# A Fourier mixing layer and a mixture of experts on one core: where token numbers are copied, how the set-up is ordered, and what a block load waits for

## The chip, the cores and the metric

The kernel runs on one core of one Trainium2 chip. The metric is device time in microseconds (us), the median of several runs. PE is the matrix engine, DVE the vector engine, ACT the scalar engine, POOL is GpSimd, and SP is the engine that here only issues DMAs. Each engine takes its instructions strictly in the order in which the built program lists them, so one that waits holds up everything listed behind it.

## The reference

```python
B, S, D, E, F = 8, 2496, 256, 8, 1024
X = np.fft.rfft(x, axis=1)                       # x: (B, S, D)
y = np.fft.irfft(X * (filt_r + 1j * filt_i)[None], n=S, axis=1)
t = y.reshape(B * S, D)                          # 19968 tokens
logits = t @ w_gate + modality_bias[modality_id]
e_idx = np.argmax(logits, axis=1)
gate_w = softmax(logits)[np.arange(B * S), e_idx]
for e in range(E):
    mask = e_idx == e
    out[mask] = gate_w[mask, None] * (np.maximum(t[mask] @ w1[e], 0.0) @ w2[e])
```

## The kernel before

**Mixing.** Each of the eight batches goes through three matrix stages that together are the transform, the filter and the transform back. Stage 1 (`stage1`, tiles `fp`/`ps`, `t`) writes to DRAM (`b1_d`), stage 2 (`stage2`) loads it again (`load_t2`), multiplies by the filter on DVE (`p<-xf,g` with the real part `g1`, `xf<-xf,g` with the imaginary part `g2`) and by two constant matrices `a1m` and `a2m` (`pz`), and writes `z` to DRAM (`b2_d`). Stage 3 (`stage3`) loads that (`load_t4`), leaves the mixed tokens in `yo` with the token's number behind the row, and makes the router's logits.

**Routing.** For each batch `count` and `place` find every token's expert and its place in that expert's bin, `scatter` writes the rows into `bins_d` in DRAM with 20 indirect DMAs from POOL, and `table` lists on DVE which blocks of 256 rows are full by now. A round is the list of blocks that one batch's table opens: rounds 0 to 6 have 5, 10, 10, 10, 9, 10 and 10 blocks, known before the data, and the last one has the rest (15 of them in the main part, so 79 blocks in all; a branch behind it takes more where there are more).

**Experts.** For each block `load` issues on SP a DMA of 256 rows with their token numbers and gates into `xs` (five buffers, at most three blocks loaded ahead). `turn` copies the expert's `w1` into `w` and the last two words of each row into `meta` on DVE, turns the rows on PE (`pT`) and copies them on DVE into `xT`. `up` is four groups of matmuls `hps` with an ACT evacuation into `hT`; `down` is four groups into `ops`, two DVE evacuations into `osb` (three buffers; `ops` has two) and two indirect DMAs from POOL into the output. The expert steps are interleaved with the next batches' stages; up to some step of the front, `busy` matmuls that compute nothing fill PE.

**What sets the order.** The program is written with the stages interleaved by step number `n`; a scheduling layer then lists each engine's instructions and puts in the waits for data. Two of its calls matter here. `tc.issue_after(x)` puts an instruction behind `x` in the list. `free_of(ins, group)` says that `ins` need not wait for the members of `group`, because they touch other rows. Before the change a block load was not freed of the scatters (group `bins`), so it waited for every scatter that stands ahead of it in the program, those of later batches too. The set-up is listed by hand, inside `tc.manual_schedule()`.

Of the kernel before, what the change touches and what calls it, by code (L numbers as in the profile page):

```python
# [20 lines left out]
P = 128  # L21
# [7 lines left out]
def kernel(  # L29
# [202 lines left out]
    with tc.manual_schedule():  # L232
# [25 lines left out]
        nc.sync.dma_start(mb_sb, moe_modality_bias.rearrange("a e -> (a e)")[None, :])  # L258


        rows = row_int([], rows_i, "rows")
        bit0 = row_int([(ALU.bitwise_and, 1)], rows_i, "bit0")
        half = row_int([(ALU.arith_shift_right, 1)], rows_i, "half")
# [70 lines left out]
        for s0 in range(0, NS, SPB):  # L334
            for src, dst in ((w2m, a1m), (w2x, a2m)):
                tp = pp.tile([P, EV * D], F32, tag="ps", name="tp")
                for i in range(SPB):
                    nc.tensor.matmul(tp[:KB, i * KB:(i + 1) * KB], lhsT=src[:, s0 + i, :], rhs=perm,
                                     start=True, stop=True)
                ev = nc.vector.tensor_copy if dst is a1m else nc.scalar.copy  # L340
                ev(dst[:, s0:s0 + SPB, :].rearrange("p s c -> p (s c)"), tp[:KB, 0:SPB * KB])
            if s0 == 0:
                nc.vector.tensor_scalar_mul(a1m[:, 0, :], a1m[:, 0, :], wt0[:KB])
        for ga, gb in ((1, 8), (8, 16), (16, NS)):
            nc.vector.tensor_scalar_mul(g2[:, ga:gb, :], g2[:, ga:gb, :], sgn[:KB])


        zs = col("zs", lambda t: nc.vector.tensor_single_scalar(t, quart, 0.0, op=ALU.is_equal))
# [24 lines left out]
        for b in range(3):  # L373
            mv = mrawc[:, b].rearrange("p g (t two) -> p g t two", two=2)
            nc.vector.tensor_copy(mids[KA:P, :, b:NYF:3], mv[KA:P, :, 3:4 * NYG:4, 0])
        nc.vector.memset(ones_sq, 1.0)

        eio_i = const_pool.tile([P, E], I32)
        nc.gpsimd.iota(eio_i, pattern=[[1, E]], base=0, channel_multiplier=0)
# [212 lines left out]
    def scatter(g, t):  # L592

        rows = P if t < NYF else KA
        with behind("out", 1):
            ins = nc.gpsimd.indirect_dma_start(  # L596
                out=bins_d[:, :], out_offset=IOA(ap=st[g]["pos"][:rows, t:t + 1], axis=0),
                in_=st[g]["yw"][:rows, t, :], in_offset=None)

        free_of(ins, "bins")  # L600
        free_of(ins, "bin_reads")
        tc.add_to_no_dep_group("bins", ins.ins)
        paced(ins)

    def paced(ins):
        tc.add_manual_dep(ins.ins, marks["pe"][-1].name,
                          mybir.DependencyInfo(mybir.DependencyClass.Sync, mybir.DependencyReason.DATA),
                          reason="pace")
# [2 lines left out]
        tc.declare_no_dep(ins.ins, group=group, reason="disjoint rows")  # L611


    def table(K, last):

        b2 = [P, K, E]
        ni = tp_.tile([P, E], I32, tag="ni")
        av = tp_.tile([P, E], F32, tag="av")
        if last:
            ts(av, cnt, 1.0, float(BLK - 1))  # L620
            nc.vector.tensor_copy(ni, av)
        else:
            nc.vector.tensor_copy(ni, cnt)
        nc.vector.tensor_single_scalar(ni, ni, int(math.log2(BLK)), op=ALU.arith_shift_right)
        nc.vector.tensor_copy(av, ni)
        nc.vector.tensor_sub(av, av, done)
        incl = tp_.tile([P, E], F32, tag="incl")
        nc.vector.tensor_tensor_scan(incl, ones_sq[:, 0:E], av, 0.0, op0=ALU.mult, op1=ALU.add)
        excl = tp_.tile([P, E], F32, tag="excl")
        nc.vector.tensor_sub(excl, incl, av)  # L630
        v = tp_.tile([P, E], F32, tag="v")
        nc.vector.tensor_sub(v, done, excl)
        m = tp_.tile(b2, F32, tag="m")
        jb = jio[:, 0:K, None].to_broadcast(b2)
        nc.vector.tensor_tensor(m, incl[:, None, :].to_broadcast(b2), jb, op=ALU.is_le)
        ej = tp_.tile([P, K], F32, tag="ej")
        nc.vector.reduce_sum(ej, m, axis=AX.X)
        ec = tp_.tile([P, K], F32, tag="ec")
        nc.vector.tensor_scalar_min(ec, ej, float(E - 1))
        ej_i = tp_.tile([P, K], I32, tag="eji", bufs=3)  # L640
        nc.vector.tensor_copy(ej_i, ec)
        nc.vector.tensor_tensor(m, eio[:, None, :].to_broadcast(b2), ej[:, :, None].to_broadcast(b2),
                                op=ALU.is_equal)
        tmp = tp_.tile(b2, F32, tag="mt")
        nc.vector.tensor_mul(tmp, m, v[:, None, :].to_broadcast(b2))
        lb = tp_.tile([P, K], F32, tag="lb")
        nc.vector.reduce_sum(lb, tmp, axis=AX.X)
        nc.vector.tensor_add(lb, lb, jio[:, 0:K])
        bj = tp_.tile([P, K], F32, tag="bj")
        nc.vector.scalar_tensor_tensor(bj, in0=ej, scalar=float(BPE), in1=lb, op0=ALU.mult, op1=ALU.add)  # L650
        nc.vector.tensor_scalar_min(bj, bj, float(E * BPE))
        bj_i = tp_.tile([P, K], I32, tag="bji", bufs=3)
        nc.vector.tensor_copy(bj_i, bj)
        if last:
            left_i = const_pool.tile([1, 1], I32, name="left_i")
            nc.vector.tensor_copy(left_i, incl[0:1, E - 1:E])
            return ej_i, bj_i, left_i
        else:
            ts(excl, excl, -1.0, float(K))
            nc.vector.tensor_scalar_max(excl, excl, 0.0)  # L660
            nc.vector.tensor_tensor(excl, excl, av, op=ALU.min)
            nc.vector.tensor_add(done, done, excl)
            return ej_i, bj_i

    binv = bins_d.rearrange("(n p i) d -> n p i d", p=P, i=NI)

# [5 lines left out]
    def load(tab, j):  # L672

        ej_i, bj_i = tab[:2]
        with behind("ld", 2):
            bj = nc.values_load(bj_i[0:1, j:j + 1], engines=(ET.SP,), min_val=0, max_val=E * BPE)
        xs = ep.tile([P, NI, RW], I32, tag="xs", bufs=5)
        ld = nc.sync.dma_start(xs, binv[ds(bj, 1)].rearrange("o p i d -> p (o i) d"))
        tc.add_to_no_dep_group("bin_reads", ld.ins)
        marks["ld"].append(ld.ins)  # L680
        return dict(xs=xs, ej_i=ej_i[0:1, j:j + 1])
# [6 lines left out]
    def turn(b):  # L688

        xh = b["xs"].bitcast(BF16)  # L690
        with behind("w1", 1):
            ej = nc.values_load(b["ej_i"], engines=(ET.DVE,), min_val=0, max_val=E - 1)
        b["w1"] = ep.tile([P, DC, F], BF16, tag="w1", name="w1")
        cp = nc.vector.tensor_copy(b["w1"].rearrange("p a f -> p (a f)"),  # L694
                              w1sb[:, ds(ej, 1)].rearrange("p o a f -> p (o a f)"))
        marks["w1"].append(cp.ins)
        b["xT"] = ep.tile([P, DC, NI, P], BF16, tag="xT", name="xT")

        b["meta"] = ep.tile([P, NI, 2], I32, tag="meta", bufs=8, name="meta")
        nc.vector.tensor_copy(b["meta"], b["xs"][:, :, DW:DW + 2])  # L700
        pT = op.tile([P, DC, NI, P], BF16, tag="tr")
        for dc in range(DC):
            for i in range(NI):
                nc.tensor.transpose(pT[:, dc, i, :], xh[:, i, dc * P:(dc + 1) * P], ident)  # L704
        nc.vector.tensor_copy(b["xT"], pT)  # L705
        b["hT"] = ep.tile([P, FT, NI * P], BF16, tag="hT", name="hT")

    FQ = 2
# [142 lines left out]
    while True:  # L851
        for g in range(1, B):
            if 0 <= n - begin[g] < NP:
                input_piece(g, n - begin[g])
        for g in range(B):
            k = n - begin[g] - OFF2
            if (k + LEAD) % 4 == 0 and 0 <= k + LEAD < NS // EV:
                load_t2(g, (k + LEAD) // 4)
            if 0 <= k <= NS // EV:
                stage2(g, k)  # L860
        for g in range(B):
            k = n - begin[g] - OFF3
            if (k + LEAD) % 3 == 0 and 0 <= k + LEAD < NPY:
                load_t4(g, (k + LEAD) // 3)
            if 0 <= k <= NPY + 1:
                stage3(g, k)
            if k == NPY + 2:
                count(g)
            if k == NPY + 3:
                place(g)  # L870
                tabs[g] = table(KR[g], g == B - 1)
                to_bins.append([g, 0])
        alone[0] = n < FRONT
        if alone[0]:
            busy(10 if n < NP + 18 else 4)
        left = 2 if n < begin[B - 1] + OFF3 + NPY + 3 else NY
        left = pace(pace(left) if n < FRONT + 10 else left)
        if n >= WSTART and n % 3:
            load_w()
        owed += STEPS  # L880
        while owed >= 1:
            owed -= 1
            outs = len(marks["out"])
            moe.step()
            if len(marks["out"]) == outs:
                left = pace(left)
        n += 1
        if not to_bins and n > begin[B - 1] + OFF3 + NPY + 4:
            break
    LAG = 0  # L890
    while moe.step():
        pass
    left = nc.values_load(tabs[B - 1][2], min_val=0, max_val=LEFT)  # L893
    for p0, p1 in zip(PARTS[1:], PARTS[2:]):
        with tc.If(left > p0):
            for m in marks.values():
# [35 lines left out]
```

## Time and profile before

| | |
|---|---|
| median of 3 runs | 711.7 us (709.67 to 718.71) |
| the profiled execution | 709.73 us, its span 707.6 us |
| PE busy | 580.3 us, 82% of the span |
| DVE, ACT, POOL busy | 369.9, 379.9 and 365.8 us |
| mean granted TensorE clock | 0.913 of full speed |

The span runs from the first to the last instruction; 2.1 us lie around it. Busy time counts work and not the waits between. The granted clock takes two values, 1.0 (2.4 GHz) and 0.5 (1.2 GHz), so a mean between them says how much of a stretch ran at each. Times in a timeline count from the start of the span.

### The profile page before, as it was taken

What the parts mean: (1) busy time and instruction counts of PE and PEld (TensorE: products, weight loads), DVE (VectorE), ACT (ScalarE), POOL (GpSimd) and SP (SyncE); (2) the same over time, 40 slices, a digit from 0 to 9 for tenths busy, and PEclk for the clock granted to TensorE, in tenths of its full rate; (3) what the DMA queues carried; (4) which work ended last, traced back from release to release, by engine and by line L of the source; (5) the groups of instructions that cost most, each with busy time, mean ns of one, the idle gap of its engine ahead of it and who ended that gap; (6) DMA issues with size and microseconds to landing.
All of it is one profiled execution on the core that took longest, in us unless ns stands there. A gap on an engine that the chain in (4) does not pass through costs nothing. (4 is left out here: it accounts for less than half of the span.)

```text
span 707.6 us, 16119 instructions
## 1 busy us (share of the span) xinstructions
PE 580.3 (82%) x4966; PEld 485.0 (69%) x4966; DVE 369.9 (52%) x1225; ACT 379.9 (54%) x672; POOL 365.8 (52%) x409
## 2 busy tenths in 40 slices
PE   3738678796997899898989979899869359999990
PEld 2527566565776688686878868687658249999990
DVE  8252134574655656564486557456446135555540
ACT  4414455564575577674767746454435126666660
POOL 8002111175376367376647727756766755555451
PEclk9969778898799699998999999899999799999996
DMA  9969889997767767656675565344223333333320
GB/s 154 227 132 201 178 226 210 224 244 180 187 177 176 188 165 184 191 132 179 161 194 151 160 168 136 116 112 137 91 89 107 103 104 102 106 113 101 97 76 20
DMA packets 84222, 106.08 MB, mean 150 GB/s; under 512 B 12164, under 2 KB 66250, under 8 KB 83980
## 3 DMA queue, kind: packets, MB, share of 16 engines
q0 software_dynamic: 21504, 50.75, 29.7%
q1 hardware_dynamic: 62632, 54.23, 29.1%
q8 instruction: 48, 0.79, 0.5%
q14 instruction: 38, 0.31, 0.1%
HBM read 71.07 MB, written 52.74 MB: 175 GB/s over the span
## 5 line engine op out<-in xcount | busy, mean ns | idle before, releaser
L720 ACT ACTIVATE hT<-hps 128x512 f16<-128x512 f32 x316 | 188.3, 597 | 174.6 <-PE hps L715 173.6
L715 PE MATMUL hps<-xT,w 128*128 128x256 f16 x1264 | 208.6, 286 | 33.5 <-DVE xT L705 33.2
L737 POOL DMA_INDIRECT out_dram<-osb,meta x158 | 158.5, 1003 | 126.6 <-DVE osb L735 73.1
L596 POOL DMA_INDIRECT bins_d<-yo,pos_i x160 | 162.1, 1013 | 77.9 <-issue 31.1
L728 PE MATMUL ops<-w2sb,hT 128*128 x1264 | 197.3, 279 | 0.3 <-issue 0.2
L715 PEld LDWEIGHTS <-w 128*128 128x128 f16 x1264 | 146.4, 148 | 45.8 <-DVE xT L705 36.1
L728 PEld LDWEIGHTS <-hT 128*128 128x128 f16 x1264 | 126.2, 100 | 15.7 <-issue 0.6
L700 DVE COPY meta<-xs 128x4 int32<-128x4 int32 x79 | 14.8, 188 | 120.5 <-DMA xs<-bins_d 110.6
L477 ACT CAST xf<-ps 104x512 f16<-104x512 f32 x96 | 56.2, 585 | 34.4 <-PE ps L464 32.2
L479 DVE TENSOR_TENSOR p<-xf,g 104x512 f16<-104x512 f16 x96 | 40.5, 422 | 63.8 <-ACT xf L477 63.4
L735 DVE TENSOR_SCALAR osb<-ops,meta 128x256 f32<-128x256 f32 x158 | 69.3, 475 | 5.5 <-PE ops L728 5.5
L694 DVE COPY w<-w1sb 128x2048 f16 x79 | 55.3, 700 | 28.5 <-PE hps L715 26.1
L486 ACT CAST z<-pz 104x512 f16<-104x512 f32 x96 | 56.6, 590 | 23.3 <-PE pz L473 12.5
L472 PE MATMUL pz<-p,a1m 104*104 104x256 f16 x192 | 52.2, 290 | 12.1 <-DVE p L479 4.1
L464 PE MATMUL ps<-t,w2m 104*104 104x256 f16 x192 | 41.1, 299 | 24.7 <-DMA t<-b_d 21.4
L473 PE MATMUL pz<-xf,a2m 104*104 104x256 f16 x192 | 51.0, 289 | 0.2 <-DVE xf L480 0.2
L824 PE MATMUL busy<-ident 128*128 128x256 f16 x296 | 50.9, 310 | 0.0
L205 ACT CAST t<-fp 96x512 f16<-96x512 f32 x57 | 32.3, 583 | 33.6 <-PE fp L200 19.8
L705 DVE COPY xT<-pT 128x512 f16<-128x512 f16 x79 | 33.1, 419 | 19.9 <-PE pT L704 19.5
L464 PEld LDWEIGHTS <-w2m 104*104 104x104 f16 x192 | 24.7, 139 | 26.4 <-issue 21.4
L533 DVE COPY yT<-lt 128x512 f16<-128x512 f16 x80 | 33.5, 419 | 17.0 <-PE lt L529 14.1
L480 DVE TENSOR_TENSOR xf<-xf,g 104x512 f16<-104x512 f16 x96 | 40.2, 419 | 2.2 <-DVE p L479 0.3
(194 smaller groups left out, 716.5 us busy)
## 6 DMA issues: line engine op xcount, KB each, us to landing
xs<-bins_d SPq DMA_DIRECT2D x79, 130.0 KB
t<-b_d SPq DMA_DIRECT2D x24, 416.0 KB
b_d<-z SPq DMA_DIRECT2D x48, 208.0 KB
xt<-in_x_dram POOLq DMA_DIRECT2D x24, 384.0 KB
b_d<-t SPq DMA_DIRECT2D x48, 192.0 KB
t<-b_d SPq DMA_DIRECT2D x24, 384.0 KB
w1sb<-in_moe_w_dram POOLq DMA_DIRECT2D x16, 256.0 KB
w2sb<-in_moe_w_dram POOLq DMA_DIRECT2D x8, 512.0 KB
```

The costliest lines, as they stand in the source:

```text
L464: mm = nc.tensor.matmul(ps[:KB, i, :], lhsT=w2m[:, s + i, :], rhs=st[g]["t2", s // SCH][:, s % SCH + i, :], start=True, stop=True)
L472: nc.tensor.matmul(pz[:KB, i, :], lhsT=a1m[:, s_ + i, :], rhs=p1[:, i, :], start=True, stop=False)
L473: nc.tensor.matmul(pz[:KB, i, :], lhsT=a2m[:, s_ + i, :], rhs=p2[:, i, :], start=False, stop=True)
L477: nc.scalar.copy(xf, ps[:KB])
L486: nc.scalar.copy(st[g]["z"][:, kk % 2], pz[:KB])
L596: ins = nc.gpsimd.indirect_dma_start(out=bins_d[:, :], out_offset=IOA(ap=st[g]["pos"][:rows, t:t + 1], axis=0), in_=st[g]["yw"][:rows, t, ...
L694: cp = nc.vector.tensor_copy(b["w1"].rearrange("p a f -> p (a f)"), w1sb[:, ds(ej, 1)].rearrange("p o a f -> p (o a f)"))
L715: mm = nc.tensor.matmul(hps[:, k, :], lhsT=b["w1"][:, dc, ft:F:FT], rhs=b["xT"][:, dc].rearrange("p i t -> p (i t)"), start=(dc == 0), sto ...
L720: nc.scalar.activation(b["hT"][:, q * FQ:(q + 1) * FQ, :], hps, AF.Relu)
L728: nc.tensor.matmul(b["ops"][:, i, :], lhsT=b["hT"][:, ft, i * P:(i + 1) * P], rhs=w2sb[:, ds(b["ej"], 1), ft, :], start=(ft == 0 and i == ...
L735: nc.vector.tensor_scalar_mul(osb[:, i, :], b["ops"][:, i, :], gate[:, i, :])
L737: ins = nc.gpsimd.indirect_dma_start(out=out[:, :], out_offset=IOA(ap=b["meta"][:, i, 0:1], axis=0), in_=osb[:, i, :], in_offset=None, bou ...
```

## The change

Four edits. In the set-up, `ones_sq` is filled as the first of the hand-listed DVE instructions and no longer near their end; and the sign `sgn`, which was multiplied into `g2` on DVE in three instructions, is put on the rows of `a2m` instead, by the ACT copies that write `a2m` out of PSUM anyway (the first slot keeps a plain copy, so one copy becomes two). In `turn`, the `meta` copy stands behind the `xT` copy and not ahead of it. And a block load of the round that batch g opened is freed of the scatters of the batches after g; the last round waits for all, as before.

```diff
+        nc.vector.memset(ones_sq, 1.0)
         rows = row_int([], rows_i, "rows")
...
-                ev = nc.vector.tensor_copy if dst is a1m else nc.scalar.copy
-                ev(dst[:, s0:s0 + SPB, :].rearrange("p s c -> p (s c)"), tp[:KB, 0:SPB * KB])
+                if dst is a1m:
+                    nc.vector.tensor_copy(dst[:, s0:s0 + SPB, :].rearrange("p s c -> p (s c)"),
+                                          tp[:KB, 0:SPB * KB])
+                    continue
+                a = 0
+                if s0 == 0:
+                    nc.scalar.copy(dst[:, 0, :], tp[:KB, 0:KB])
+                    a = 1
+                nc.scalar.activation(dst[:, s0 + a:s0 + SPB, :].rearrange("p s c -> p (s c)"),
+                                     tp[:KB, a * KB:SPB * KB], AF.Copy, scale=sgn[:KB])
...
-        for ga, gb in ((1, 8), (8, 16), (16, NS)):
-            nc.vector.tensor_scalar_mul(g2[:, ga:gb, :], g2[:, ga:gb, :], sgn[:KB])
...
-        nc.vector.memset(ones_sq, 1.0)
...
+        tc.add_to_no_dep_group("bins%d" % g, ins.ins)
...
         ld = nc.sync.dma_start(xs, binv[ds(bj, 1)].rearrange("o p i d -> p (o i) d"))
+        for h in range(tab[2] + 1, B):
+            free_of(ld, "bins%d" % h)
...
-        b["meta"] = ep.tile([P, NI, 2], I32, tag="meta", bufs=8, name="meta")
-        nc.vector.tensor_copy(b["meta"], b["xs"][:, :, DW:DW + 2])
         pT = op.tile([P, DC, NI, P], BF16, tag="tr")
...
-        nc.vector.tensor_copy(b["xT"], pT)
+        turned = nc.vector.tensor_copy(b["xT"], pT)
+        b["meta"] = ep.tile([P, NI, 2], I32, tag="meta", bufs=8, name="meta")
+        with tc.issue_after(turned.ins):
+            nc.vector.tensor_copy(b["meta"], b["xs"][:, :, DW:DW + 2])
```

The order tables below are of the built programs: line, operation, output and inputs, shape. In the first, DVE's list in the last round's neighbourhood, where batch 7 is scattered; before:

```order
L735 TENSOR_SCALAR osb<-ops,meta 128x256 x2
L692 TENSOR_LOAD ej_i
L692 ISA x2
L700 COPY meta<-xs 128x4
L705 COPY xT<-pT 128x512
L700 COPY meta<-xs 128x4
L694 ISA
L694 COPY w_9594<-w1sb 128x2048
L735 TENSOR_SCALAR osb<-ops,meta 128x256 x2
L692 TENSOR_LOAD ej_i
L692 ISA x2
L700 COPY meta<-xs 128x4
```

and after:

```order
L745 TENSOR_SCALAR osb<-ops,meta 128x256 x2
L701 TENSOR_LOAD ej_i
L701 ISA x2
L712 COPY xT<-pT 128x512
L715 COPY meta<-xs 128x4
L703 ISA
L703 COPY w_9592<-w1sb 128x2048
L745 TENSOR_SCALAR osb<-ops,meta 128x256 x2
L701 TENSOR_LOAD ej_i
L701 ISA x2
L712 COPY xT<-pT 128x512
L715 COPY meta<-xs 128x4
```

Before, a `meta` copy stands one or two blocks ahead of the `xT` copy of its own block; now it stands right behind it, everywhere.

The second is SP's list in the same place, each block load with its waits (DMASW are the semaphores of POOL's DMAs, the scatters among them; DMAHW those of SP's own; PE and DVE free the `xs` buffer). Before:

```order
L678 DMA xs_9418<-bins_d 128x260 [waits DMASW4_49,DMASW3_49,DMASW5_49,DMASW0_49,DMAHW1_49,DVE_49,PE_49]
L676 TENSOR_LOAD bj_i_7091
L676 ISA x2
L751 TENSOR_LOAD end_i_9719
L751 ISA x2
```

and after:

```order
L685 DMA xs_9416<-bins_d 128x260 [waits DMAHW4_49,DMAHW7_49,DVE_49,PE_49]
L683 TENSOR_LOAD bj_i_7089
L683 ISA x2
L685 ISA
L685 DMA xs_9515<-bins_d 128x260 [waits DMAHW0_49,DVE_49,PE_49]
```

The DMASW waits are gone from this load; in the whole list they are left on the first load of each round.

The third is DVE's list in the set-up; before:

```order
L341 CAST a1m<-tp 104x416 x5
L345 TENSOR_SCALAR g_69<-g_69,sgn 104x1792
L345 TENSOR_SCALAR g_69<-g_69,sgn 104x2048 x2
L348 TENSOR_SCALAR zs<-quart 128x1
L349 TENSOR_TENSOR zri<-zs,bit_147 128x1
```

and after, where `g_69` is `g2`:

```order
L371 TENSOR_SCALAR wbm<-wb_400,j0w 96x48
L372 TENSOR_SCALAR wbm<-wb_400,j1w 96x48
L486 TENSOR_TENSOR xf<-xf,g_69 104x512 x2
L377 CAST mids<-mraw 96x8x6 x3
L378 CAST mids<-mraw 96x8x2
```

The first DVE instruction that needs `g2` was ahead of all the small constants, and of `ones_sq`; now it is the filter's own product, with the first stage-2 evacuations ahead of it and about half of the constants (`eio` among them) still behind.

## Rows read from the trace of the kernel before

**Rows 1.** The page's busy table: busy us, share of the span, instructions.
```profile
PE 580.3 (82%) x4966; PEld 485.0 (69%) x4966; DVE 369.9 (52%) x1225; ACT 379.9 (54%) x672; POOL 365.8 (52%) x409
```

**Rows 2.** Waits over the whole span: us in total, times, longest us.
```profile
DVE meta L700 <- DMA xs<-bins_d: 110.6, 41, 8.0
...
PE ps L464 <- DMA t<-b_d: 21.4, 5, 8.7
```

**Rows 3.** Waits of SP's queue over the whole span.
```profile
SPq L678 <- DMA bins_d<-yo,pos_i: 189.3, 54, 15.1
...
SPq L678 <- PE pT L704: 57.4, 26, 3.2
```

**Rows 4.** Waits of PE from 237 to 580 us.
```profile
PE hps L715 <- DVE xT L705: 33.2, 9, 10.9
PE pz L472 <- DVE yo L539: 3.5, 1, 3.5
PE pz L472 <- DVE lg L542: 2.5, 1, 2.5
PE ps L464 <- DVE lg L542: 2.2, 1, 2.2
PE lt L524 <- DVE yo L539: 1.9, 1, 1.9
```

**Rows 5.** Timeline, 540 to 561 us: start, us, instruction, idle before it.
```profile
546.97 0.38 PE L704 MATMUL pT<-ident,xs 128*128 128x128 f16 x4
...
549.89 0.17 DVE L700 COPY meta<-xs 128x4 int32<-128x4 int32 x1 [6.05 <-DMA xs<-bins_d]
...
557.00 0.35 SPq L678 DMA_DIRECT2D xs<-bins_d  x1
...
559.44 0.17 DVE L700 COPY meta<-xs 128x4 int32<-128x4 int32 x1 [7.96 <-DMA xs<-bins_d]
559.52 0.42 DVE L705 COPY xT<-pT 128x512 f16<-128x512 f16 x1
...
560.00 1.07 PE L715 MATMUL hps<-xT,w 128*128 128x256 f16 x4 [10.89 <-DVE xT L705]
```

**Rows 6.** Busy time by stretch, the granted clock (PEclk) and the DMA share behind it.
```profile
554.40:564.60 10.20, 4.61 (x24) 3.55 (x25) 1.88 (x5) 1.19 (x2) 7.92 (x8) 0.50 0.27 80
...
sum 41.00, PE 34.47 PEld 25.76 DVE 24.54 ACT 13.32 POOL 22.16; mean PE 4.31 PEld 3.22 DVE 3.07 ACT 1.66 POOL 2.77
...
sum 17.20, PE 11.61 PEld 9.02 DVE 7.00 ACT 3.58 POOL 10.38; mean PE 3.87 PEld 3.01 DVE 2.33 ACT 1.19 POOL 3.46
```

**Rows 7.** The same by batch: PE, PEld, DVE, ACT, POOL, each with its instructions.
```profile
301.40:366.70 65.30, 60.41 (x513) 49.27 (x512) 38.14 (x133) 41.51 (x75) 40.09 (x42) 0.92 0.66 168
...
483.50:537.50 54.00, 44.47 (x409) 36.11 (x408) 28.44 (x106) 22.43 (x38) 35.76 (x36) 0.97 0.26 82
537.50:577.00 39.50, 21.54 (x177) 18.15 (x174) 11.25 (x36) 11.94 (x20) 29.57 (x30) 0.87 0.36 111
```

**Rows 8.** The same for a stretch of experts alone.
```profile
590.00:680.00 90.00, 90.00 (x864) 84.53 (x862) 49.00 (x117) 57.04 (x96) 46.42 (x49) 1.00 0.32 102
```

**Rows 9.** What POOL waited for, 537.5 to 577 us.
```profile
POOL bins_d L596 <- issue: 2.1, 7, 0.3
```

**Rows 10.** Timeline of the set-up.
```profile
41.55 2.01 DVE L345 TENSOR_SCALAR g<-g,sgn 104x1792 f16<-104x1792 f16 x3 [11.92 <-DMA g<-g]
...
47.45 0.60 PE L409 MATMUL mb_ps<-mb_sb,ones_sq 1*128 1x16 f32 x2 [12.31 <-DVE ones_sq L376]
...
47.68 1.11 POOL L435 DMA_DIRECT2D w1sb<-in_moe_w_dram  x2 [12.97 <-DVE eio L381]
...
51.21 0.42 PE L473 MATMUL pz<-xf,a2m 104*104 104x256 f16 x1
```

**Rows 11.** Busy time by stretch around the end of the set-up.
```profile
44.00:48.00 4.00, 0.56 (x3) 0.52 (x3) 3.32 (x26) 0.80 (x2) 0.32 (x1) 0.50 0.00 0
...
53.00:142.00 89.00, 67.94 (x535) 54.98 (x532) 32.95 (x100) 45.72 (x84) 14.50 (x28) 0.85 0.97 208
```

More of the change, by code (lines that the diff above doesn't have):

```diff
@@ L611, in free_of, with table @@
         tc.declare_no_dep(ins.ins, group=group, reason="disjoint rows")
-    def table(K, last):
+    def table(g, K, last):
         b2 = [P, K, E]
@@ L656, in table @@
             nc.vector.tensor_copy(left_i, incl[0:1, E - 1:E])
-            return ej_i, bj_i, left_i
+            return ej_i, bj_i, B - 1, left_i
         else:
@@ L662, in table @@
             nc.vector.tensor_add(done, done, excl)
-            return ej_i, bj_i
+            return ej_i, bj_i, g
     binv = bins_d.rearrange("(n p i) d -> n p i d", p=P, i=NI)
@@ L870 @@
                 place(g)
-                tabs[g] = table(KR[g], g == B - 1)
+                tabs[g] = table(g, KR[g], g == B - 1)
                 to_bins.append([g, 0])
@@ L892 @@
         pass
-    left = nc.values_load(tabs[B - 1][2], min_val=0, max_val=LEFT)
+    left = nc.values_load(tabs[B - 1][3], min_val=0, max_val=LEFT)
     for p0, p1 in zip(PARTS[1:], PARTS[2:]):
```

## The prediction

> **What bounds the kernel now.** I read the page first, then the waits, then the stretches where they lie. PE is busy 82% of the span, far more than any other engine [rows 1]; so time is gained where PE stands still or runs slowly, and nowhere else. The list of waits shows that the largest wait for data on DVE is the `meta` copy for its block load: 110.6 us in 41 times [rows 2]. SP has the cause: its block loads wait 189.3 us in 54 times for scatters into the bins [rows 3]. Neither engine is the bound, so these sums are not time yet. What they cost is in PE's own waits from 237 to 580 us: 33.2 us in nine waits for an `xT` copy and four single ones of 3.5, 2.5, 2.2 and 1.9 us behind other DVE instructions, 43.3 us together [rows 4].
>
> The timeline shows how one arises [rows 5]. PE turned the rows of a block at 546.97; their `xT` copy needed nothing more. But DVE's list has the `meta` copies of two later blocks ahead of it. The second one's load went out at 557.00, once scatters of batch 7 had landed that this block does not hold, and its `meta` ran at 559.44, after 7.96 us of standing. `xT` followed at 559.52, and PE began again at 560.00 after 10.89 us. The turned block had been there for 12 us.
>
> A stop costs more than itself. In the eight stretches of half clock that stand beside these stops, PE was busy for 34.47 us at a granted clock of 0.5, which is 17.2 us lost; three of the eight lie behind 483.5 us, with 11.61 us busy, so 5.8 us of the 17.2 are there and 11.4 before [rows 6].
>
> **The bins.** A block load of rounds 0 to 6 no longer waits for scatters of later batches; the order table shows the waits gone. It adds no instruction. What is left to wait for is the `xs` buffer, and the first load of each round, which waits for its own batch. The loads go out early, three blocks ahead; a block lasts 3.75 us where only experts run (864 matmuls in 90 us, 36 for a block, so 24 blocks) [rows 8], so a load has some 11 us of cover, and one that had nothing to wait for took 2.4 us to its `meta` (557.00 to 559.44) [rows 5].
>
> Against this edit speaks a rule of the Trainium skill, DMA: Bandwidth & Descriptors, section Issuing engines are not separate DMA queues: transfers from SP and POOL run on the same 16 DMA engines and interleave, so loads that no longer wait for scatters run beside them. From rows the engines are 66% busy in one batch's stretch and 26 and 36% in the last two [rows 7], so there is room, and a load would have to take over four times its 2.4 us to be seen: by the rows this costs 0. [...]
>
> **The `meta` copy** moves behind `xT`. It takes what stood ahead of `xT` away, so that even a late load stops only its own block. Both edits remove the same stops; I count them once. The copy is 0.17 us [rows 5], 79 of them 13.4 us. It used to run while DVE waited anyway; now it can hold the next DVE instruction up. Bounds: 0 and 13.4 us. DVE is busy 38.14 of 65.30 us in a full batch [rows 7], so most of it stays hidden; I take 3. It also frees `xs` 0.6 us after the turn and not before it, which the cover of three blocks hides.
>
> **The stops removed, in two parts.** The last two stretches, 483.5 to 577 us, have PE idle for 54.00 − 44.47 = 9.5 and 39.50 − 21.54 = 18.0 us [rows 7], 27.5 together; so 43.3 − 27.5 = 15.8 us of the DVE stops lie earlier.
>
> *Early, 237 to 483.5:* 15.8 us of stops and 11.4 us of clock, 27.2 us. Is another engine next? In the fullest batch POOL has 42 instructions, 40.09 us [rows 7], and 0.3 us between two even where it is never idle [rows 9]: 40.1 + 12.6 = 52.7 us of 65.3. PE's 60.41 us at a mean clock of 0.92 are 55.6 at full clock [rows 7]. POOL is close but below. I take all 27.2.
>
> *Late, 483.5 to 577:* PE could give 27.5 + 5.8 = 33.3 us, but POOL holds that up. Its 36 and 30 instructions need 35.76 + 10.8 = 46.6 and 29.57 + 9.0 = 38.6 us, 85.2 of the 93.5 us: it can gain 8.3 [rows 7, 9]. Beyond that PE can only run ahead of the output DMAs. `osb` has three buffers and `ops` two, so `down` of a block may begin when the output of the fifth block before it has left; in the trace it is the block just before. That lead is four blocks of 3.75 us, 15.0 us, and POOL works it off later, when a block costs it less than PE (46.42 us busy of 90, [rows 8]). So 8.3 + 15.0 = 23.3 us, the smaller of the two.
>
> **The set-up.** `ones_sq` is filled early, and the three sign products go (2.01 us on DVE, behind 11.92 us of waiting for the copied half of `g2`). Now PE waits 12.31 us for `ones_sq`, since every small constant is listed behind those products [rows 10]. With them gone PE goes on to stage 2 when its load lands; but the filter's product with `g2` cannot begin before 41.55, when `g2` is there. Today the first `pz` from it is at 51.21. So at most 51.21 − 41.55 = 9.7 us. The lower bound is 0: stage 1 of batch 1 is now listed behind those first stage-2 matmuls. The row nearest to the value is that of the DMA engines: 97% busy from 53 to 142 us, and idle from 44 to 48 [rows 11], because the weight loads wait for `eio`, 12.97 us [rows 10]. Where transfers bound the next 89 us, the idle 4.0 us is what an earlier start gives. I take 4. The added ACT copy costs nothing: ACT is busy 0.80 us in those 4 [rows 11].
>
> **The sum** against the profiled execution's 709.7 us (2.0 below the median, within the runs' scatter): 27.2 + 23.3 + 4.0 − 3.0 = 51.5, which gives 658 us.
>
> **The rivals.**
>
> *POOL binds and gives no lead.* If an output DMA's landing is late, or DVE stops at an `osb` copy whose buffer has not come free, and stops with it `xT` behind it, the 15.0 us of lead go: 658 + 15 = 673 us. For it: POOL does not rest from 537.5 to 577 beyond the 0.3 us between instructions. Against: five buffers lie between the two.
>
> *The stops move.* The first load of a round still waits for its batch's scatters, which a busy POOL does late, and SP holds the `z` stores and stage loads behind it. If half of the stops comes back so, 25 of the 50.5 us: 658 + 25 = 683 us. For it: PE already waits 21.4 us for stage loads [rows 2]. Against: blocks are queued up when a round opens.
>
> *Slower.* The loads now reach SP's front early and wait there for an `xs` buffer; in the trace such waits are up to 3.2 us, 57.4 in all [rows 3], mostly in the last stretch where nothing is behind them. If they stood in front of stage stores and loads twice in each of six batches, each would cost a stage-load wait of 4.3 us (21.4 in 5, [rows 2]) and as much half clock as the stops had on average, 17.2 of 43.3 or 1.7 us: 12 × 6.0 = 72 us, 658 + 72 = 730 us. It decides when a load's buffer comes free later than the next `z` is ready. Against: the block five before is turned two blocks before the load is listed.
>
> That the change does not do what it says is excluded by the order table.
>
> **How the numbers follow.** The forecast has 0.53, POOL without lead 0.25, stops that move 0.15, slower 0.05, and 0.02 something else. Faster by over 2%, below 697 us, holds the first two, most of the third and nothing of the fourth: 0.88. Within 2%, about what a measurement can tell from no change, 0.07; slower 0.05. Range: the lower end takes the set-up's full 9.7 (5.7 more), no cost of the `meta` copy (3) and all 33.3 of the late stops (10): 640. The upper end is the case of moved stops with the set-up's 0 (4 us) and 3 more for `meta`: 690.
>
> **What would show it.** Of the waits: DVE's `meta` for `xs` near zero, SP's waits for scatters down to the first load of each round, PE's for `xT` a few us. Of the stretches: full clock from about 240 us on; POOL without rest over the last two batches, and `osb` or `out_dram` waits there if it binds. In the set-up: no wait for `ones_sq`, the first `pz` at 42 to 46 us, no empty DMA stretch. I am wrong if PE's idle time between 240 and 580 us stays above 30 us, or if POOL's share says that it could not go faster.

## The result and the profile after

The changed kernel takes 675.6 us (median of 4 runs, 669.94 to 689.98) where the kernel before takes 711.4 in the same comparison: a ratio of 0.945, 95% interval 0.9345 to 0.9559. The ratio is taken from the runs within 1.5% of each kernel's fastest, so it is not quite that of the two medians. The profiled execution is 669.94 us, its span 668.2. The range of 640 to 690 holds it; the forecast of 658 is 12 us too low against the profiled execution (18 against the median), and the time lies next to the rival in which POOL gives no lead (673).

The page's busy table answers to [rows 1]; PE has 565.7 us of work where it had 580.3, with the same number of instructions, because less of it runs at half clock (the mean granted clock is 0.928, it was 0.913):

```profile
PE 565.7 (85%) x4966; PEld 475.1 (71%) x4966; DVE 370.7 (55%) x1222; ACT 379.7 (57%) x673; POOL 367.8 (55%) x409
```

Three milestones split the gain: the first scatter of batch 2, the first of batch 6, and the end of PE's last matmul. Before they stand at 237.1, 483.5 and 690.3 us, after at 237.4, 462.7 and 650.9. So the front lost 0.3, the early stretch gained 21.1 (246.4 to 225.3) and the late one 18.6 (206.8 to 188.2); the sum, 39.4, is the whole difference of the spans.

PE's waits from 237 to 580 us, which answer to [rows 4]: 43.3 us there behind DVE, here 18.9 in all, and none above 4.3.

```profile
PE hps L725 <- DVE xT L712: 11.0, 6, 3.7
PE ps L517 <- ACT t L205: 4.3, 1, 4.3
PE psO L578 <- DVE c L569: 2.1, 3, 0.8
PE ops L738 <- issue: 1.5, 5, 0.5
```

SP's waits over the whole span answer to [rows 3]. The block loads still stand 172.6 us, but now for the `xs` buffer, which the `meta` copy frees; for scatters they wait five times, about once for each round's first load. The `meta` wait for `xs`, 110.6 us in [rows 2], has no row any more. In its place DVE has a new one, the last line here (of the list of all engines):

```profile
SPq L685 <- DVE meta L715: 172.6, 54, 7.8
...
SPq L685 <- DMA bins_d<-yo,pos_i: 16.5, 5, 8.6
...
DVE osb L745 <- DMA out_dram<-osb,meta: 23.0, 7, 6.9
```

The stretches answer to [rows 7]: us, then PE, PEld, DVE, ACT and POOL with their instructions, granted clock, DMA share, GB/s. The first one is the whole early part, the last one the early part of the kernel before. In the second and third, POOL's work and 0.3 us for each of its instructions are 36.4 + 11.1 = 47.5 of 47.4 us and 31.5 + 9.6 = 41.1 of 40.9: it never rests.

```profile
237.40:462.70 225.30, 217.53 (x1981) 181.58 (x1980) 154.44 (x521) 154.06 (x278) 149.95 (x153) 0.98 0.66 176
...
462.70:510.10 47.40, 46.13 (x445) 38.74 (x444) 33.30 (x121) 24.47 (x43) 36.41 (x37) 1.00 0.35 104
510.10:551.00 40.90, 30.97 (x246) 26.14 (x243) 13.04 (x34) 16.50 (x28) 31.45 (x32) 0.87 0.35 111
...
237.10:483.50 246.40, 228.50 (x1979) 187.57 (x1978) 151.36 (x523) 155.32 (x279) 149.66 (x152) 0.94 0.61 162
```

Where the late time stays is seen in three timelines of 519 to 529 us, DVE's, POOL's and PE's (start, us, instruction, idle before it). POOL issues the two output DMAs of a block at 523.44 and 524.73, after four scatters in a row; the `osb` copies wait 5.66 us for that buffer and begin at 527.28. `xT`, whose block had been turned at 522.90, stands behind them and runs at 528.23, and PE goes on at 528.71 after 3.67 us.

```profile
519.61 0.88 DVE L745 TENSOR_SCALAR osb<-ops,meta 128x256 f32<-128x256 f32 x2 [2.42 <-DMA out_dram<-osb,meta]
...
527.28 0.88 DVE L745 TENSOR_SCALAR osb<-ops,meta 128x256 f32<-128x256 f32 x2 [5.66 <-DMA out_dram<-osb,meta]
528.23 0.42 DVE L712 COPY xT<-pT 128x512 f16<-128x512 f16 x1
...
522.17 0.97 POOL L602 DMA_INDIRECT bins_d<-yo,pos_i  x1 [0.30 <-issue]
523.44 0.98 POOL L747 DMA_INDIRECT out_dram<-osb,meta  x1 [0.30 <-PE pT L711]
524.73 0.98 POOL L747 DMA_INDIRECT out_dram<-osb,meta  x1 [0.30 <-DMA bins_d<-yo,pos_i]
...
522.90 0.38 PE L711 MATMUL pT<-ident,xs 128*128 128x128 f16 x4
...
528.71 1.07 PE L725 MATMUL hps<-xT,w 128*128 128x256 f16 x4 [3.67 <-DVE xT L712]
```

The windows with half clock that are left behind 237 us answer to [rows 6]; 14.47 us busy there where it was 34.47:

```profile
295.70:302.50 6.80, 5.17 (x24) 3.37 (x24) 3.54 (x20) 2.75 (x5) 3.88 (x4) 0.50 0.73 225
527.80:534.60 6.80, 5.89 (x30) 4.55 (x31) 1.48 (x4) 1.79 (x3) 5.28 (x6) 0.50 0.25 78
538.00:541.40 3.40, 3.40 (x21) 2.64 (x19) 0.23 (x1) 1.19 (x2) 2.48 (x4) 0.51 0.29 82
sum 17.00, PE 14.47 PEld 10.56 DVE 5.25 ACT 5.73 POOL 11.64; mean PE 4.82 PEld 3.52 DVE 1.75 ACT 1.91 POOL 3.88
```

In the set-up the steps came as foreseen, and without their fruit. These are stretches that answer to [rows 11], and four instructions that answer to [rows 10], of PE's, DVE's and POOL's timelines. The first `pz` from `g2` is at 42.83 (it was at 51.21), and the DMA engines no longer stand empty from 44 to 48; but their idle time has only been spread over 36 to 53 us. The weight loads go out at 48.36, later than before (47.68), and `eio` is cast at 47.85 (before, at 47.42), with the filter's products ahead of it on DVE. The load of the next `xt` has to wait 23.96 us for PE's stage 1, which now stands behind stage 2's first matmuls, and goes out at 42.35; before it did at 34.12.

```profile
36.00:44.00 8.00, 7.33 (x51) 5.86 (x50) 1.37 (x8) 2.98 (x6) 0.59 (x1) 0.77 0.77 142
44.00:48.00 4.00, 4.00 (x39) 3.75 (x38) 1.97 (x8) 2.48 (x6) 0.00 (x0) 1.00 0.53 121
48.00:53.00 5.00, 4.96 (x46) 4.52 (x44) 4.09 (x23) 3.67 (x8) 3.74 (x7) 1.00 0.72 116
53.00:142.00 89.00, 59.66 (x452) 46.50 (x450) 28.87 (x88) 39.84 (x74) 12.09 (x23) 0.81 0.94 205
...
42.83 0.27 PE L479 MATMUL pz<-xf,a2m 104*104 104x256 f16 x1 [0.67 <-DVE xf L486]
...
47.85 0.17 DVE L387 CAST eio<-eio_i 128x8 f32<-128x8 int32 x1
...
42.35 0.59 POOL L137 DMA_DIRECT2D xt<-in_x_dram  x1 [23.96 <-PE fp L200]
48.36 1.11 POOL L441 DMA_DIRECT2D w1sb<-in_moe_w_dram  x2 [5.43 <-DVE xf L486]
```

### The profile page after: what moved, and what is told of

Same layout as the page of the kernel before. It is cut to its first block, busy times and chain, and to the rows that moved or that the text cites. A ratio compares the mean times of both kernels' runs of the same rounds, so it can differ in the third digit from the quotient of the medians.

```text
span 668.2 us, 16107 instructions
## 1 busy us (share of the span) xinstructions
PE 565.7 (85%) x4966; PEld 475.1 (71%) x4966; DVE 370.7 (55%) x1222; ACT 379.7 (57%) x673; POOL 367.8 (55%) x409
## 4 chain that ended last, share of the span: by engine, by line
PE 54%; DMA 20%; issue 10%; POOL 5%; DVE 5%; ACT 3%; POOLq 0%; SPq 0%; DVEq 0%; ACTq 0%
PE hps L725 15%; PE ops L738 13%; DMA t<-b_d 7%; DMA b_d<-t 7%; POOL out_dram L747 5%; PE ps L517 4%; PE ps L518 4%; PE lt L530 3%; PE busy L834 3%; DMA bins_d<-yo,pos_i 2%; PE pz L479 2%; PE pz L478 2%; PE ps L470 2%; PE pT L711 2%; DMA g<-g 2%
## 5 line engine op out<-in xcount | busy, mean ns | idle before, releaser
L730 ACT ACTIVATE hT<-hps 128x512 f16<-128x512 f32 x316 | 188.3, 597 | 144.6 <-PE hps L725 143.5
L725 PE MATMUL hps<-xT,w 128*128 128x256 f16 x1264 | 203.5, 281 | 11.1 <-DVE xT L712 11.0
L747 POOL DMA_INDIRECT out_dram<-osb,meta x158 | 160.6, 1016 | 91.4 <-DVE osb L745 43.1
L738 PE MATMUL ops<-w2sb,hT 128*128 x1264 | 193.8, 276 | 1.5 <-issue 1.5
L738 PEld LDWEIGHTS <-hT 128*128 128x128 f16 x1264 | 124.8, 99 | 15.7 <-issue 2.3
L478 PE MATMUL pz<-p,a1m 104*104 104x256 f16 x192 | 50.4, 282 | 6.6 <-DVE p L485 6.3
L479 PE MATMUL pz<-xf,a2m 104*104 104x256 f16 x192 | 48.9, 280 | 2.1 <-DVE xf L486 1.9
L470 PEld LDWEIGHTS <-w2m 104*104 104x104 f16 x192 | 24.0, 136 | 37.1 <-issue 27.2
L518 PEld LDWEIGHTS <-wbm 96*32 96x32 f16 x160 | 14.8, 93 | 39.4 <-issue 30.1
```

The source lines that it names most:

```text
L470: mm = nc.tensor.matmul(ps[:KB, i, :], lhsT=w2m[:, s + i, :], rhs=st[g]["t2", s // SCH][:, s % SCH + i, :], start=True, stop=True)
L478: nc.tensor.matmul(pz[:KB, i, :], lhsT=a1m[:, s_ + i, :], rhs=p1[:, i, :], start=True, stop=False)
L479: nc.tensor.matmul(pz[:KB, i, :], lhsT=a2m[:, s_ + i, :], rhs=p2[:, i, :], start=False, stop=True)
L725: mm = nc.tensor.matmul(hps[:, k, :], lhsT=b["w1"][:, dc, ft:F:FT], rhs=b["xT"][:, dc].rearrange("p i t -> p (i t)"), start=(dc == 0), sto ...
L730: nc.scalar.activation(b["hT"][:, q * FQ:(q + 1) * FQ, :], hps, AF.Relu)
L738: nc.tensor.matmul(b["ops"][:, i, :], lhsT=b["hT"][:, ft, i * P:(i + 1) * P], rhs=w2sb[:, ds(b["ej"], 1), ft, :], start=(ft == 0 and i == ...
```

## The experiments

Ratios are to the kernel before on the same chip, with 95% intervals; the first four runs shared one chip, the next four another, and the last two pairs one each.

### One part of the change at a time

**The set-up alone** (`e1_setup`): the kernel before with the first four pieces of the diff, up to the second `ones_sq` line, and nothing else.

> The kernel before with the two set-up edits alone. Theory (the front is bound by the bytes it moves, and no load starts earlier): the first scatter stays at 142 us within 1 us and the time within 3 us of before, ratio 0.997 to 1.003. Rival (the forecast's term): 4 us less, 0.994 or lower, with the first scatter at 138 us or earlier.

Measured: 715.83 us beside 713.16, ratio 1.003 (0.9981 to 1.0081), the `xT` stops still 30.6 us in 7. Alone it gains nothing, and the interval leaves out the rival's 0.994. The first scatter, at 146.7 us, is where neither expectation had it: 5 us later than the 141.7 of the kernel before, in one execution each (more on this moment below).

**The `meta` copy alone** (`e2_meta`):

```diff
-        b["meta"] = ep.tile(...)
-        nc.vector.tensor_copy(b["meta"], b["xs"][:, :, DW:DW + 2])
...
+        turned = nc.vector.tensor_copy(b["xT"], pT)
+        b["meta"] = ep.tile(...)
+        with tc.issue_after(turned.ins):
+            nc.vector.tensor_copy(b["meta"], b["xs"][:, :, DW:DW + 2])
```

> The kernel before with the meta copy behind the xT copy alone; the block loads still wait for all scatters ahead of them. Theory (DVE's place in line is what stopped PE, the late loads stop it only once the three blocks ahead are used up): most of the gain up to batch 6, 15 to 21 us, and some 7 us in the last two batches: 23 to 29 us less, ratio 0.959 to 0.968. Rival (the load's wait is the cause): PE's stops move to the turned rows and under 10 us are gained, 0.985 or higher.

Measured: 691.49 us, ratio 0.972 (0.9621 to 0.9822), some 20 us, between the two expectations. PE's waits from 237 to 580 us have no `xT` stop. PE now stops one step earlier, where it turns a block whose load is late (first line); the loads still stand for scatters (second line, of SP's).

```profile
PE pT L702 <- DMA xs<-bins_d: 15.0, 5, 5.6
...
SPq L678 <- DMA bins_d<-yo,pos_i: 172.0, 53, 10.0
```

So with the copy out of the way a late load still costs PE: 15.0 us here, in five stops. The prediction's "stops only its own block" put no price on that.

**The freed loads alone** (`e3_bins`):

```diff
         tc.add_to_no_dep_group("bins", ins.ins)
+        tc.add_to_no_dep_group("bins%d" % g, ins.ins)
...
+        for h in range(tab[2] + 1, B):
+            free_of(ld, "bins%d" % h)
```

> The kernel before with the block loads freed alone; meta stays ahead of xT. Theory (either edit removes the same stops, since a load that goes out early has landed when its meta copy is listed): 34 to 40 us less, ratio 0.944 to 0.953, DVE's wait of meta for xs under 15 us. Rival (both are needed): meta still waits over 50 us and under 20 us are gained, 0.972 or higher.

Measured: 693.42 us, ratio 0.975 (0.9653 to 0.9849), some 18 us. My theory that either edit alone removes the stops fell here. The rival's two numbers came. The wait for scatters is down to 19.6 us in 6, but the `meta` copy, still ahead of `xT`, stands 73.6 us (it was 110.6), for something new: `meta` has eight buffers, and the one that it needs is still to be read by output DMAs that have not run. PE's `xT` stops stay at 14.1 us in 7.

```profile
DVE meta L703 <- DMA out_dram<-osb,meta: 73.6, 31, 7.4
...
PE hps L718 <- DVE xT L708: 14.1, 7, 3.8
```

**The freed loads with 24 `meta` buffers** (`e7_metabufs`), to see whether that row is the cause:

```diff
-        b["meta"] = ep.tile([P, NI, 2], I32, tag="meta", bufs=8, name="meta")
+        b["meta"] = ep.tile([P, NI, 2], I32, tag="meta", bufs=24, name="meta")
```

> The kernel before with the freed block loads alone, as in the earlier run of that edit, and 24 buffers for meta instead of 8. Theory (with loads early, the meta copy stands ahead of the xT copy only because its eight buffers wait for output DMAs, 73.6 us in 31): that wait falls below 10 us, and the edit then does nearly all that both do, a ratio to the kernel before of 0.945 to 0.958. Rival (the meta copy ahead of the xT copy meets some other late thing): the meta copy waits as long for something else, and the ratio stays at 0.970 to 0.980.

Measured: 676.35 us, ratio 0.942 (0.9378 to 0.947), as good as the whole change. The `meta` wait for output DMAs has no row; what is left of the copy's waiting for its load is below, with the `osb` wait that the whole change has too:

```profile
DVE osb L738 <- DMA out_dram<-osb,meta: 20.9, 4, 6.9
DVE meta L703 <- DMA xs<-bins_d: 15.6, 11, 4.0
```

So the freed loads are enough for the whole gain, on condition that the `meta` copy doesn't stop DVE for its own buffer. Moving the copy and giving it buffers are two ways to that, equal within their intervals.

### The late stretch

**A fourth `osb` buffer** (`e4_osb`), with `xs` cut from five to four for room:

```diff
-        xs = ep.tile([P, NI, RW], I32, tag="xs", bufs=5)
+        xs = ep.tile([P, NI, RW], I32, tag="xs", bufs=4)
...
-        osb = ep.tile([P, NI, D], F32, tag="osb", bufs=3)
+        osb = ep.tile([P, NI, D], F32, tag="osb", bufs=4)
```

> The changed kernel with four osb buffers for three, and four xs buffers for five to make room. Theory (the late stops come from DVE standing at an osb copy whose buffer is still being written out, with the xT copy behind it): one more block of lead, 3 to 6 us less than the changed kernel, DVE's osb wait for output DMAs down from 23.0 us to under 18, PE's stops at xT down from 11.0 us. Rival (POOL's rate alone sets that stretch, buffers do not matter): the same time within 2 us. With four xs buffers costing something: up to 3 us more.

Measured: 669.89 us, ratio 0.936 with a wide interval (0.9164 to 0.9559): in the direction expected, and not to be told from the whole change by that alone. DVE's `osb` wait is 17.7 us in 5 and PE's `xT` stops are 8.0 us in three, both down as expected.

**The last batch's scatters spread** (`e5_spread`), two for each block in place of about five:

```diff
+    steps = 0
...
-        left = pace(pace(left) if n < FRONT + 10 else left)
+        tail = n >= begin[B - 1] + OFF3 + NPY + 3
+        if not tail:
+            left = pace(pace(left) if n < FRONT + 10 else left)
...
-            if len(marks["out"]) == outs:
+            steps += 1
+            if len(marks["out"]) == outs if not tail else steps % 2 == 0:
                 left = pace(left)
```

> The changed kernel, with the scatters of the last batch listed at two for each block of experts instead of about five. Theory (in the last round osb's copies wait for output DMAs that stand behind clumps of scatters on POOL, and hold the xT copy behind them): the xT stops of PE behind 510 us, 10.2 us in four, fall below 4, and the half clock beside them, 4 to 5 us lost, mostly goes; the ratio to the kernel before falls from 0.945 to 0.925 to 0.935. Rival (POOL's rate sets the time whatever the order): PE stands still elsewhere, and the ratio stays at 0.940 to 0.950.

Measured: 673.83 us, ratio 0.938 (0.9327 to 0.944), between the two expectations; the interval touches the ratio of the whole change. The stops did not go: eight of them, 9.6 us together, the `osb` wait 21.9 us in 8. The clumps alone are not the cause.

**Both** (`e8_best`):

> The changed kernel with the last batch's scatters spread as in the run beside it, and four osb and four xs buffers. If the spreading takes the stops and the fourth buffer takes what is left (alone it gave a ratio to the kernel before of 0.936), a ratio of 0.920 to 0.930; if both take the same stops, that of the better of the two, 0.930 to 0.937; if POOL's rate binds, 0.936 to 0.945.

Measured: 661.18 us, ratio 0.920 (0.9148 to 0.9258), the best version. From the first scatter of batch 7 to PE's end it takes 131.8 us; the whole change takes 140.8, the spread scatters 137.6 and the fourth buffer 137.4, in one execution each. So the two together give more than either alone, which the ratio says too: its interval lies below that of the spread scatters and that of the whole change (the fourth buffer's is too wide to tell). PE's waits from 470 to 600 us and the last two scatter stretches:

```profile
PE hps L725 <- DVE xT L712: 5.9, 4, 2.3
...
464.40:512.30 47.90, 46.76 (x450) 39.31 (x448) 33.92 (x124) 24.98 (x44) 36.96 (x36) 1.00 0.33 102
512.30:564.50 52.20, 47.25 (x442) 43.00 (x442) 24.09 (x60) 29.23 (x49) 40.30 (x39) 1.00 0.41 122
```

POOL rests as little as before (40.3 + 11.7 = 52.0 of 52.2 us). What changed is the order of its work and how far PE may run ahead of it: PE is busy 47.3 of 52.2 us there, at full clock (30.97 of 40.9 us in the whole change).

### The front

**Eight more weight loads** (`e6_twice`):

```diff
+            if q < DC and e < E // 2:
+                paced(nc.gpsimd.dma_start(w1sb[:, E - 1 - e, q], moe_w1[e, q * P:(q + 1) * P, :]))
             if q < DC:
                 ins = nc.gpsimd.dma_start(w1sb[:, e, q], moe_w1[e, q * P:(q + 1) * P, :])
```

> The changed kernel, with eight more weight loads of 256 KB in the front, the same data into places that a later load fills again. Theory (the front is bound by its transfers, so an earlier start of PE gains nothing there): 2.1 MB at the rate of the stretch from 53 to 142 us, 208 GB/s, put the first scatter 8 to 10 us later than the 142.4 of the changed kernel, and the whole time is 7 to 10 us longer, a ratio to the kernel before of 0.955 to 0.960. Rival (the front is bound by its chain of waits, transfers have room): first scatter within 3 us of 142.4 and the ratio within 0.940 to 0.950.

Measured: 683.41 us, ratio 0.952 (0.9465 to 0.9581), 5 us above the whole change's ratio, though the two intervals overlap; first scatter at 152.0, where three kernels with nothing added on the same chip have 144.6, 148.3 and 148.6. The DMA share from 53 to 142 us went to 1.00:

```profile
53.00:142.00 89.00, 56.11 (x418) 43.71 (x417) 24.78 (x68) 33.93 (x63) 15.26 (x30) 0.81 1.00 210
```

2.1 MB, some 10 us of transfer, cost about 5 by either measure (4.8 us from the mean of those three): about half of it seems to have found room. Neither expectation holds whole.

**Half of the weights not loaded** (`e9_half`), the places of experts 4 to 7 filled with zeros on POOL, so that those experts' outputs are zero:

```diff
-            if q < DC:
+            if e >= E // 2:
+                ins = nc.gpsimd.memset(w1sb[:, e, q] if q < DC else w2sb[:, e], 0.0)
+            elif q < DC:
```

> The changed kernel without the weights of experts 4 to 7: their places are filled with zeros by POOL and not loaded, so 4.2 MB fewer come in the front, and the outputs of those experts are zero. Theory (the front is bound by its transfers): the engines' share from 53 to 142 us was 0.94 and 4.2 MB are 20 us at 208 GB/s; the first scatter comes 8 to 20 us earlier than in the changed kernel and its kin (142 to 148 us), and the whole time is 8 to 20 us shorter, a ratio to the kernel before of 0.917 to 0.934. Rival (the chain of stores, loads and copies from stage to stage sets the front's length): first scatter at 140 or later and a ratio of 0.938 to 0.948.

This run and the next fell on a chip where the kernel before takes 791.75 us (below), so its ratio, 0.975 (0.9697 to 0.9798), doesn't compare with those above. The front does: first scatter at 135.7 us, where kernels that load all their weights on the two slower chips have 140.2, 141.2 and 145.1. The share from 53 to 142 us is 0.83:

```profile
53.00:142.00 89.00, 64.09 (x477) 50.37 (x475) 33.17 (x110) 41.89 (x77) 23.94 (x29) 0.78 0.83 187
```

Not all of the 4.2 MB would have come before the first scatter. Up to that moment this kernel moved 24.6 MB (135.7 us at 181 GB/s, first line) and `e10_nosetup`, with all its weights on the same chip, 27.3 MB (141.2 us at 193 GB/s):

```profile
0.00:135.70 135.70, 90.00 (x668) 73.67 (x668) 58.24 (x206) 65.32 (x118) 39.48 (x67) 0.88 0.85 181
...
0.00:141.20 141.20, 90.59 (x664) 73.83 (x665) 60.56 (x209) 64.61 (x117) 32.88 (x68) 0.85 0.93 193
```

So the 20 us of the expectation are some 13 there (2.7 MB at 208 GB/s), and they bring the batch 4 to 9 us forward, at the low end of the theory or below it. Transfers are a part of the front's bound. That the chain from stage to stage is the rest is likely and not shown.

### The set-up again, and two slower chips

**The best version without the set-up's edits** (`e10_nosetup`; then `e11_without`, with `e12_with` beside it, the best version itself). The edit is the diff's set-up part, taken out.

> The kernel with spread scatters and four osb and four xs buffers, without the set-up's edits. Theory (they are worth nothing, since they bring no transfer forward): the same as with them, a ratio to the kernel before of 0.915 to 0.926. Rival (they were hidden by noise or by the stops that stand behind, and are worth the 4 us of the forecast): 0.926 to 0.932.

> The same kernel as in the earlier run without the set-up's edits (spread scatters, four osb and four xs buffers), beside the one with them on the same chip. Theory (the set-up's edits bring no transfer forward and are worth nothing): the two medians within 0.5% of each other, some 3.5 us, and the first scatters within 4 us. Rival (worth the 4 us of the forecast or more): this one 4 us or more above the other, and its first scatter as much later.

> The kernel with spread scatters, four osb and four xs buffers and all edits of the change, beside the one without the set-up's edits. [...] Rival: 4 us or more below the other.

Measured: `e10_nosetup` 779.72 us beside 791.75, ratio 0.977 (0.9706 to 0.9826), which tells nothing of the set-up for want of a partner. On the third chip the kernel before takes 799.18; without the set-up's edits 787.60, ratio 0.986 (0.9819 to 0.9898), with them 789.78, ratio 0.990 (0.9855 to 0.9935), so this chip gives the change even less than the other slower one, where `e10_nosetup` had 0.977. The difference of 2.2 us is 0.3%, and against the edits. Their first scatters, 145.1 without and 140.2 with, are 4.9 apart, as the rival had it; but that moment moves by more than this among kernels with the same front. Over all profiled executions with the usual weights the six without the edits have 141.2 to 148.6, mean 144.95, and the six with them 140.2 to 148.3, mean 144.95.

## Why the prediction was right, and where not

**The bound and the cause** hold. PE's stops behind DVE's `meta` copy were the time to be had: 43.3 us of waits became 18.9 and half clock fell with them. The rule that the prediction set beside this (the Trainium skill, DMA: Bandwidth & Descriptors, Issuing engines are not separate DMA queues) is that transfers of SP and POOL share the 16 DMA engines and interleave. Here the DMA share of the early part rose from 0.61 to 0.66, and PE has no wait for `xs` between 237 and 580 us, so no cost of that sharing is seen in the block loads.

**"Both edits remove the same stops; I count them once"** gave the right sum for a wrong reason. Either alone gains 18 to 20 us, and together 39: moved alone, the copy leaves PE waiting for late rows; freed alone, the loads put the copy into a wait for its own buffer. The prediction looked at what the copy reads and not at what it overwrites. `e7_metabufs` shows that what the freed loads lacked was `meta` buffers: one number changed, and the row and the missing half of the gain came together.

**Early, 27.2 less 3 for the copies = 24.2:** measured 21.1. What is missing is one stop of 4.28 us at 297.3 with the half clock beside it (5.17 us busy, so 2.6 lost), 6.9 together; 21.1 + 6.9 = 28.0 is the term without the 3. That it fits so closely is in part luck: a half-clock window of the kernel before that ran on to 243.7 us, with 5.56 us busy behind 237.1 and so 2.8 lost, is not among the prediction's eight, and the changed kernel has none behind 237.7 until 295.7. The stop at 297 is the rival of stops that move, once, and SP's and ACT's rows (waits from 277 to 291 us, then two timelines) show how it came about:

```profile
SPq L685 <- DMA bins_d<-yo,pos_i: 4.8, 1, 4.8
...
SPq L461 <- DMA b_d<-z: 3.0, 1, 3.0
...
283.04 1.35 SPq L685 DMA_DIRECT2D xs<-bins_d  x2
286.07 0.37 SPq L494 DMA_DIRECT2D b_d<-z  x1
289.55 0.34 SPq L461 DMA_DIRECT2D t<-b_d  x1
...
290.38 0.34 SPq L208 DMA_DIRECT2D b_d<-t  x1
...
284.00 0.58 ACT L205 CAST t<-ps 96x512 f16<-96x512 f32 x1
...
296.69 0.58 ACT L205 CAST t<-ps 96x512 f16<-96x512 f32 x1 [4.27 <-DMA b_d<-t]
```

SP stood 4.8 us for the scatters that the first load of a round needs. Behind that load came another one, a `z` store, a stage load that waited 3.0 us for this store to land, and only then, at 290.38, a `t` store whose data ACT had written by 284.58. ACT's `t` copy at 296.69 needs the buffer which that store reads, and waited 4.27 us for it. No run takes the wait of the first load away, so that the stop would go with it is read from these times and not tested. The `meta` copy's own 3 us are seen nowhere: the version that leaves it ahead of `xT` is no faster.

**Late, 23.3, the smaller of POOL's 8.3 + 15.0 and PE's 33.3:** measured 18.6. PE's bound was right: 18.6, the 11.0 us of `xT` stops left, all of which lie here, and half of the (5.89 + 3.40) us at half clock are 34.3. The lead of four blocks was mis-sized: with POOL's 8.3 taken as it stands, 10.3 of its 15.0 us came. (The two stretches of scatters themselves became 5.2 us shorter, 93.5 to 88.3, with 69 instructions of POOL in them for 66.) "`down` of a block may begin when the output of the fifth block before it has left" is true of the buffers. But the copy into the third `osb` buffer is listed on DVE ahead of the next block's `xT`, so that a full `osb` stops PE by way of `xT` and before `down`: this is the rival without lead, in part. One buffer and another order of POOL's list gave back 9.0 us in the profiled executions, with POOL as busy as ever, and the intervals of the two ratios, 0.945 and 0.920, lie apart; that is the shown part. How much of it is the lead's length and how much the clumps is not settled, since neither alone stands clear of the whole change's interval.

**The set-up, 4 us:** measured 0. The step that failed is "where transfers bound the next 89 us, the idle 4.0 us is what an earlier start gives". The loads that could have filled the idle stretch went out later and not earlier, the one of `xt` by 8.2 us and the first of the weights by 0.7; only those behind them came sooner (the second `xt` load at 51.53, before at 59.76). By their rows two things made them late, and both were known: stage 1 is listed behind stage 2's first matmuls, the reason given for the lower bound, and `eio` behind the filter's products, as the text under the third order table says. And transfers bound the front only in part: adding and leaving out some moved the first scatter by about half of their time (4.8 us for 10, 4 to 9 for 13, one execution each). Which weighs more was not settled.

**Loads that wait for `xs` in front of the stages**, the prediction's slower rival, cost nothing that PE's rows show. The loads wait 172.6 us for `xs`, three times what [rows 3] had. PE's waits for stage loads over the whole span grew from 21.4 us to 29.0, but 5.1 of that is a new wait at 33.5 us, long before the first block load at 177.0, and the last of the five is at 229.4.

**The signs.** PE's idle time from 240 to 580 us is 19.6 us (45.0 before), below the 30 that would have meant a wrong prediction. Full clock from 240 us on did not come, by the three windows above. POOL without rest did, in the last two batches; that it could then go no faster, the second sign of being wrong, is answered by `e8_best`, where PE got further with POOL as busy. All three terms came out below the forecast, by 3.1, 4.7 and 4.3 us, and none above, so no errors cancelled: the range held because its upper end had room for them.

## What to carry to other kernels

Before counting two edits as two ways to the same end, run each alone, and ask of a copy that moves what it reads, what it overwrites and what stands behind it on its engine: here each edit alone stopped at the next of these. Where an engine works off a backlog without rest, the slower engine's rate is not the last word: a buffer more and an even order let the bound engine run ahead. A gap in a busy resource is worth nothing until one names the instruction that could fill it, and sees it issued sooner.

## What the runs showed that I had not expected

**The same kernel on other chips.** On two of the chips the kernel before took 791.75 and 799.18 us, where it took 711 to 719 on the others, and the best version gained 1% there and not 8%. Up to the first scatter of batch 1 these kernels keep pace (187.8 us in `e12_with`, 185.1 in `e8_best`); behind it they fall back. ACT, DVE and PE stop for 2 to 5 us with nothing that the profile can name ("remote" is a semaphore of no known sender, "issue" no wait at all), often two engines at once. Counted from 237 to 640 us, stops of over 1 us with these two names on ACT, DVE and PE are 34, with 74 us, in `e12_with`, and one, of 1.5 us, in `e8_best`, the same kernel. The timeline of `e12_with` at 620 us, in which both engines go on at the same moment, and PE after them:

```profile
620.02 0.69 DVE L703 COPY w<-w1sb 128x2048 f16 x1 [4.23 <-remote]
620.02 1.09 ACT L730 ACTIVATE hT<-hps 128x512 f16<-128x512 f32 x2 [2.34 <-remote]
...
620.67 0.60 PE L725 MATMUL hps<-xT,w 128*128 128x256 f16 x4 [1.91 <-ACT hT L730]
```

That such stops cover those which the change removes, so that it gains little there, is likely and not shown: no run takes them away. What makes them was not found. The Trainium skill (Runtime: NRT & Kernel Launch, Instruction fetch mechanics) says that each engine fetches its instructions by a DMA queue of its own, mostly hidden; the larger of the two queues that the profile calls by this name moved 48 packets and 0.79 MB in either profile, which tells nothing of whether the engines waited for it. A ratio measured on one chip is that chip's.

**The clock.** A stop's length did not decide alone whether half clock followed it: in the changed kernel the stop of 2.10 us before 537.6 was followed by 3.4 us at 0.51, and the one of 3.34 us before 546.5 by a granted clock of 1.00:

```profile
546.40:551.00 4.60, 4.04 (x36) 3.48 (x36) 1.58 (x5) 2.39 (x4) 3.69 (x4) 1.00 0.40 127
```
